# Linear attention and a two-layer block on one core: two copies of v moved behind phi(q), four transposes moved to the upper half of another PSUM bank

## The chip, the cores and the metric

The kernel runs on one core of a Trainium2 chip. The metric is the device time of one execution in microseconds (us); lower is better. The engines are named as in the profile: PE is TensorE (matrix multiplication), DVE is VectorE, ACT is ScalarE, POOL is GpSimd, SP is SyncE, which here only issues DMAs.

## The reference

```
def _attn_ref(q, k, v):                      # q, k, v: (8, 8, 576, 64)
    def phi(x):
        return np.where(x > 0, x, np.exp(x) - 1.0) + 1.0
    q_p, k_p = (phi(q), phi(k))
    kv = np.einsum('bhsd,bhse->bhde', k_p, v)
    z = np.sum(k_p, axis=2)
    num = np.einsum('bhsd,bhde->bhse', q_p, kv)
    den = np.einsum('bhsd,bhd->bhs', q_p, z)[..., None] + 1e-06
    return (num / den).astype(np.float32)

def _moe_ref(x, w_in, w_out):                # x: (4608, 512), w_in: (512, 2048)
    h = x @ w_in
    g = h - np.tanh(h)
    return (g @ w_out).astype(np.float32)    # (4608, 512)
```

The attention's result, with the heads side by side, is x. There are 8 batches of 576 tokens, 4608 rows in all.

## The kernel before, in words

**Chunks.** The 4608 rows of x are worked off in nine chunks of 512. Chunk c takes 512 rows of batch c; the last chunk takes the 64 rows that are left of each batch. A chunk has two halves. Layer 1 runs over 16 tiles `fi` of the hidden width: four matmuls each (`l1mm`, L468) into a PSUM bank, then tanh on ScalarE (L474 or L479) and a subtraction on VectorE (L475 or L480) that writes `gT`. Layer 2 runs over 16 steps `s` of four matmuls each (`l2mm`, L489), and `evac` copies its result out and stores it (L500, L513).

**The order is written by hand.** Each engine works off its instructions in the order in which the code issues them. The attention of the batches to come is placed between the matmuls by two tables of closures, `s1[fi]` and `s2[s]`: what stands in `s2[s]` is issued behind step `s` of layer 2. In chunk c the tables hold the phi work of batch c + 2 (`n2`), the numerators of batch c + 1 (`n1`) and the loads of batch c + 3; chunk 0 has entries of its own, for batches 1 and 2.

**phi.** `phi_pieces` (L137) makes, for one half `i` of a batch's heads, an exponential on ScalarE (L151), a tensor_scalar on VectorE (L152) and a minimum on VectorE (L153). `a_kphi` and `a_qphi` call it for k and q, which each have one raw buffer per pool.

**Copies of v.** `a_vp` (L201) copies half a batch of v into `vp`, the operand of the matmuls `kv_mm` (L198), beside columns of ones that give z. There is one `vp`. In chunk 1 the batch is 3, and its v is loaded by GpSimd in `s1[0]`, behind a `gate` (L482) that waits for the transposed phi(q) of batch 2.

**Numerators and kv.** `a_num(2, 3)` stands in `s2[12]` of chunk 1. It issues the numerators of batch 2 (L282, L291) and kv of batch 3 (L198), then on VectorE the copies of z and kv (`kz_copy`, L218 into `zr` and L223 into `kz`), and then `num_scale`, which multiplies the numerators by `rdb` and writes batch 2's part of `xT` (L439 four times, L444 twice). `rdb` holds the reciprocal denominators of batch 2; `a_spread` writes them to DRAM (L410) and reads them back to all partitions with two DMAs on SyncE's queue (L413). Layer 1 of chunk 2 reads that part of `xT`. `q_zb` in `s2[14]` turns `zr` by two matmuls (L230), copies the result on ScalarE (L233), and GpSimd multiplies it with phi(q) of batch 3 (L240).

**Transposes of batch 1.** In chunk 0, `s2[2]` transposes phi(q) of batch 1 on TensorE: `a_qT_pe` (L174) is called for `i` = 0 and `i` = 1, and each call issues two groups of four transposes (L182), each group into the lower half of a PSUM bank of its own, and gives back two copies into `qT` (L186), the first for ScalarE, the second for VectorE. Both copies of `i` = 0 are issued before the transposes of `i` = 1:

```
s2[2].append(lambda: ([f() for i in range(2) for f in a_qT_pe(1, i, Banks([4 + 2 * i, 5 + 2 * i]))], load_q(2)))
```

The four banks are 4, 5, 6 and 7. In layer 1 of chunk 0 the last four tiles, `fi` = 12 to 15, lie in the same four banks. All of PSUM is one tile, `ps_all`, of 8 banks of 512 float32 columns; waits between engines are put in by the framework from the accesses to it, none is written by hand.

Of the kernel before, what the change touches and what calls it, by code (L numbers as in the profile page):

```python
# [12 lines left out]
BF16 = mybir.dt.bfloat16  # L13
# [5 lines left out]
def kernel(  # L19
# [73 lines left out]
    def load(b, t, src, halves):  # L93

        n = main(b) if src is q else J
        x = src[b].rearrange("h (p j) d -> (h p) (j d)", j=J)[:, 0:n * D]
        if halves:
            y = x.rearrange("(h i q) x -> i q h x", h=2, i=2)
            for i in halves:
                for hs in ((0, 1), (1, 2)) if i and src is k and b == 0 else ((0, 2),):  # L100
                    nc.gpsimd.dma_start(out=t[:, hs[0]:hs[1], i, 0:n].rearrange("q h j d -> q h (j d)"),
                                        in_=y[i, :, hs[0]:hs[1]])
        else:
            nc.gpsimd.dma_start(out=t[:, :, :, 0:n].rearrange("q h i j d -> q (h i) (j d)"),  # L104
                                in_=x.rearrange("(n q) x -> q n x", n=4))
# [5 lines left out]
    def load_q(b):  # L111
        q_t[b] = kpool.tile([128, 2, 2, J, D], BF16, name="qraw")
        load(b, q_t[b], q, (0, 1) if b == 0 else ())
# [45 lines left out]
    def a_kphi(b, i):  # L159
        phi(b, k_t, kp_t, "kp", i)  # L160

    def a_qphi(b, i):
        phi(b, q_t, qp_t, "qp", i)

    def new_qT(b):
        qT_t[b] = work.tile([128, 2, J, 2, 64], BF16, name="qT")
# [4 lines left out]
            out=qT_t[b].rearrange("p i j g t -> p (i j) (g t)"),  # L171
            in_=qp_t[b].rearrange("p i j h d -> p (i j h d)"))

    def a_qT_pe(b, i, banks, on="AV"):  # L174
        if i == 0:
            new_qT(b)
        copies = []
        for n in range(2):
            j0, j1 = 4 * n, 4 * n + 4
            ps = banks().bitcast(BF16).rearrange("p (j t) -> p j t", t=128)  # L180
            for j in range(j0, j1):
                nc.tensor.transpose(ps[:, j - j0, :], qp_t[b][:, i, j].rearrange("p h d -> p (h d)"), ident)  # L182
            src = ps[:, 0:j1 - j0, :]
            dst = qT_t[b][:, i, j0:j1].rearrange("p j g t -> p j (g t)")
            copies.append((nc.scalar.copy if on[n] == "A" else nc.vector.tensor_copy, dst, src))
        return [lambda f=f, d=d, x=x: f(d, x) for f, d, x in copies]  # L186
# [14 lines left out]
    def a_vp(b, i, eng=nc.vector):  # L201
        eng.tensor_copy(vp[:, i, :, :, 0:64].rearrange("p j h d -> p h j d"), v_b[b % 2][:, :, i])  # L202

    def a_vp1(h, copy):
        copy(vp[:, 1, :, h, 0:64], v_b[1][:, h, 1])

    def kv_cols_mm(b, b0, o):
        kz_t[b] = kz_c[b if b < 2 else 2 + b % 2]
        kv_mm(b, lambda rs, h, i, j: vp[rs, i, j, h, :],
              lambda cs, hg, i: ps_all[cs, b0 + hg, o + 66 * i:o + 66 * i + 66])  # L210
# [67 lines left out]
    def num_mm(b, i, bank_of):  # L278

        kz, qT = kz_t[b], qT_t[b]  # L280
        for rs, cs, h, hg in quads():
            nc.tensor.matmul(ps_all[cs, bank_of(h), :].rearrange("p (j t) -> p j t", j=8), kz[rs, hg, i, 0:64],  # L282
                             qT[rs, i, 0:8, hg, :], start=True, stop=True)
# [164 lines left out]
    def new_ns(b):  # L448

        return rpool.tile([128, NP, J, 64], F32, name="ns", tag="rdb")  # L450

    def a_spread_pe(b, pairs):

        for n, p in enumerate(pairs):
            for t in range(4):
                r = slice(32 * t, 32 * t + 32)
                nc.tensor.matmul(ps_all[:, 4 + t, 128 * n:128 * n + 128], sel3[r, p].rearrange("p h e -> p (h e)"),
                                 rden_t[b][r, 0:128], start=True, stop=True)

    def a_scale(b, p, ns, n):  # L460
        nc.vector.tensor_mul(
            xT[:, p, 512 * b:512 * b + 512].rearrange("p (j t c) -> p t j c", j=8, t=4),
            ns[:, p, 0:8].rearrange("p j (t c) -> p t j c", t=4),
            ps_all[:, 4:8, 128 * n:128 * n + 128].rearrange("p t (j c) -> p t j c", c=16))
# [175 lines left out]
    for c in range(NC):  # L640
        gT = gpool.tile([128, NF, 512], BF16, name="gT")
        n1, n2 = c + 1, c + 2
        s1 = {i: [] for i in range(16)}
        s2 = {i: [] for i in range(16)}
        if c == 0:
            sub = {}

            def spread1():
                a_spread_pe(1, range(NP))
                for p in range(NP):  # L650
                    a_scale(1, p, sub["ns"], p)

            def kv1():
                kv_cols_mm(1, 4, 0)
                kz_copy(1, 4, 0)

            def num1():
                ns = sub["ns"] = new_ns(1)
                for i in (1, 0):
                    b0 = 4 + 2 * i  # L660
                    num_mm(1, i, lambda h: b0 + h)
                    nc.scalar.copy(ns[:, i::2, 0:8, :].rearrange("p a j t -> p a (j t)"), ps_all[:, b0:b0 + 2, :])

            def vp1():
                a_vp1(0, nc.vector.tensor_copy)
                a_vp1(1, nc.scalar.copy)

            s1[13].append(lambda: a_qphi(1, 0))
            s1[14].append(lambda: a_qphi(1, 1))
            s2[0].append(lambda: a_kphi(1, 0))  # L670
            s2[2].append(lambda: ([f() for i in range(2) for f in a_qT_pe(1, i, Banks([4 + 2 * i, 5 + 2 * i]))], load_q(2)))
            s2[3].append(lambda: (a_kphi(1, 1), load_k(2)))
            s2[4].append(prepare)
            s2[6].append(lambda: a_vp(1, 0))
            s2[8].append(lambda: (vp1(), load_v(2)))
            s2[9].append(kv1)
            s2[10].append(lambda: (a_den(1, 4), num1(), a_split(1)))
            s2[13].append(spread1)

            qs, ks = [], []  # L680

            def exp2(pieces, src, store, name, i):
                pieces.append(phi_pieces(2, src, store, name, i))
                pieces[i][0]()

            def rest2(f):
                f[1]()
                f[2]()

            def k2(i):  # L690
                ks.append(phi_pieces(2, k_t, kp_t, "kp", i))
                if not i:
                    ks[i][1]()

            s2[14].append(lambda: exp2(qs, q_t, qp_t, "qp", 0))
            s2[15].append(lambda: (exp2(qs, q_t, qp_t, "qp", 1), rest2(qs[0]), rest2(qs[1]), a_qT_dma(2), [f() for f in later], k2(0), k2(1)))
        elif n1 < B:
            if c == 1:
                def kv2():
                    kv_cols_mm(2, 6, 0)  # L700
                    kz_copy(2, 6, 0)

                s1[10].append(kv2)
            if n1 < QS:
                s1[11].append(lambda: (a_den(n1, 6), a_spread(n1)))
            else:
                if c == 2:
                    s1[2].append(lambda: (q_den(n1, 0, 0), q_den(n1, 0, 1)))
                e = 2 * (c == 2)
                s1[3 + e].append(lambda: q_den(n1, 1, 0))  # L710
                s1[5 + e].append(lambda: q_den(n1, 1, 1))
                s1[7 + e].append(lambda: q_scale(n1))
            m = 12 if c == 1 else 9
            if c == 3:
                s1[12].append(load_qr)
                s2[13].append(r_z)
            if c == 4:
                s2[1].append(r_phi)
                s2[12].append(r_prod)
            if c == 5:  # L720
                s2[1].append(r_scale)
            s2[m].append(lambda: (c == B - 2 and r_num(6, 128), a_num(n1, n2 if n2 < B else 0),
                                  c == B - 2 and r_copy(6, 128)))
            if n2 < B:
                s2[m + 2].append(lambda: (n2 == QS and q_zb(n2, 4), q_prod(n2)))
                if c > 1:
                    s2[15].append(lambda: (q_den(n2, 0, 0), q_den(n2, 0, 1)))
# [6 lines left out]
        if c >= 1 and n2 < B:  # L734
            d = 2
            s2[d].append(lambda: a_kphi(n2, 0))
            s2[d + 2].append(lambda: a_kphi(n2, 1))
            s2[d + 4].append(lambda: a_qphi(n2, 0))
            s2[d + 6].append(lambda: a_qphi(n2, 1))
            for i in range(2):  # L740
                s2[d + 1 + 2 * i].append(lambda i=i: a_vp(n2, i))
            if n2 + 1 < B:
                s2[15].append(lambda: (load_k(n2 + 1), load_v(n2 + 1), load_q(n2 + 1)))
        if c == 0:
# [18 lines left out]
        for fi in range(4 if c == 0 else 0, NF):  # L763
# [12 lines left out]
            elif fi % 2 and (c, fi) not in ((1, 9), (1, 11)):  # L776
                n = fi % 6
# [3 lines left out]
            if c == 1 and fi in (10, 11):  # L781
                n = 2 * (fi - 9)
                l1act2(6 + n, ps_all[:, n:n + 2, :], gT)
        os_ = {}
        for s in range(16):

            g, i = s % 4, s // 4
# [50 lines left out]
```

## Time and profile before

| What | Value |
|---|---|
| time, median of 3 runs | 282.6 us (282.32 to 282.66) |
| time of the profiled execution | 283.25 us |
| span of the profiled execution, first to last instruction | 281.4 us |
| PE busy | 275.9 us, 98% of the span |
| DVE busy | 177.9 us, 63% |
| ACT busy | 145.2 us, 52% |
| POOL busy | 82.3 us, 29% |
| granted TensorE clock, mean | 1.000 |
| layer 1, 560 matmuls of 128x512 (L468) | 123.0 us |
| layer 2, 560 matmuls of 128x512 (L489) | 124.2 us |

The span is what the trace covers; the time of the execution is 1.85 us longer. The profiled execution is one of its own and 0.65 us longer than the median of the runs. A row of a timeline reads: start in us from the span's start, length in us, engine and line, operation, output <- inputs, shape, count, and in brackets the idle time of the engine before it with what ended it. TensorE's matmuls overlap, so their pace is read from one start to the next and not from their lengths.

### The profile page before, as it was taken

How to read it: one execution, taken by the hardware profiler on the slowest of the kernel's cores; microseconds unless marked ns; L12 is line 12 of the kernel's file. 1: busy time of each engine (PE TensorE's matmuls, PEld its weight loads, DVE VectorE, ACT ScalarE, POOL GpSimd, SP SyncE). 2: the span in 40 equal slices, each digit the busy share in tenths (PEclk: the TensorE clock that was granted, in tenths of full speed). 3: DMA queues.
4: the chain of work that ended last, by engine and by line, in shares of the span. 5: the costliest groups of instructions: out<-in, count | busy, mean ns of one | idle time of the engine just before them, and what ended most of it. 6: DMA issues, size and time to landing. Idle time of an engine off the chain costs nothing.

```text
span 281.4 us, 5069 instructions
## 1 busy us (share of the span) xinstructions
PE 275.9 (98%) x2069; PEld 130.3 (46%) x2069; DVE 177.9 (63%) x289; ACT 145.2 (52%) x174; POOL 82.3 (29%) x79
## 2 busy tenths in 40 slices
PE   8999999999999999999999999999999999999995
PEld 3574544444444454444444444454444444444443
DVE  5759967993779764977497759784870267006600
ACT  4747908856246753566366735572651365126411
POOL 8652340330091409370824072505150000000000
PEclk9999999999999999999999999999999999999999
DMA  6999999799929754994498339862115210230033
GB/s 104 188 204 207 205 205 208 148 169 230 244 46 194 97 129 80 192 152 91 85 186 153 85 84 152 154 126 62 26 25 117 59 35 0 54 78 20 0 70 82
DMA packets 41559, 33.38 MB, mean 119 GB/s; under 512 B 19360, under 2 KB 37312, under 8 KB 41408
## 3 DMA queue, kind: packets, MB, share of 16 engines
q0 software_dynamic: 18688, 18.35, 40.8%
q1 hardware_dynamic: 22848, 14.71, 24.2%
q8 instruction: 16, 0.26, 0.4%
q14 instruction: 7, 0.06, 0.1%
HBM read 37.88 MB, written 9.46 MB: 168 GB/s over the span
## 4 chain that ended last, share of the span: by engine, by line
PE 69%; DMA 21%; DVE 3%; issue 2%; POOL 2%; ACT 1%; SPq 0%; POOLq 0%; DVEq 0%
PE ps_all L468 34%; PE ps_all L489 31%; DMA v<-in_v_dram 10%; DMA qraw<-in_q_dram 5%; DMA w_out_sb<-in_moe_w_out_dram 4%; DMA out_dram<-osb 3%; PE ps_all L578 2%; PE ps_all L198 1%; PE ps_all L282 1%; DVE xT L439 1%; ACT osb L500 1%; POOL w_in_sb L120 1%; DVE qp L153 1%; POOL kraw L104 1%; SPq L513 0%
## 5 line engine op out<-in xcount | busy, mean ns | idle before, releaser
L489 PE MATMUL ps_all<-w_out_sb,gT 128*128 128x512 bf16 x560 | 124.2, 379 | 0.0
L468 PE MATMUL ps_all<-xT,w_in_sb 128*128 128x512 bf16 x560 | 123.0, 379 | 0.3 <-DVE xT L439 0.3
L475 DVE TENSOR_TENSOR gT<-ps_all,th 128x1024 bf16<-128x1024 f32 x64 | 77.7, 1217 | 42.7 <-ACT th L474 42.6
L474 ACT ACTIVATE th<-ps_all 128x1024 f32<-128x1024 f32 x64 | 65.5, 1024 | 47.4 <-PE ps_all L468 47.4
L468 PEld LDWEIGHTS <-w_in_sb 128*128 128x128 bf16 x560 | 54.5, 98 | 66.3 <-issue 0.9
L489 PEld LDWEIGHTS <-gT 128*128 128x128 bf16 x560 | 54.0, 98 | 64.1 <-issue 0.2
L500 ACT COPY osb<-ps_all 128x512 f32<-128x512 f32 (+1 forms) x36 | 20.8, 582 | 55.0 <-PE ps_all L489 35.7
L240 POOL TENSOR_TENSOR pr<-qp,zb 128x1152 f32<-128x1152 bf16 x10 | 23.4, 2364 | 65.9 <-DMA zb<-zr 35.6
L254 POOL TENSOR_TENSOR qp<-qp,rd 128x1152 bf16<-128x1152 bf16 x10 | 21.0, 2112 | 28.3 <-DVE rd L251 17.9
L245 DVE TENSOR_REDUCE dn<-pr 128x9 f32<-128x576 f32 x20 | 14.5, 746 | 12.1 <-POOL pr L240 12.1
L151 ACT ACTIVATE e<-qraw 128x1152 bf16<-128x1152 bf16 (+1 forms) x16 | 18.2, 1136 | 3.6 <-DMA qraw<-in_q_dram 3.6
L151 ACT ACTIVATE e<-kraw 128x1152 bf16<-128x1152 bf16 x15 | 17.4, 1163 | 1.9 <-DMA kraw<-in_k_dram 1.9
L153 DVE TENSOR_TENSOR qp<-e,r 128x1152 bf16<-128x1152 bf16 (+1 forms) x16 | 11.9, 741 | 4.4 <-ACT e L151 3.3
L153 DVE TENSOR_TENSOR kp<-e,r 128x1152 bf16<-128x1152 bf16 x15 | 11.4, 758 | 4.3 <-ACT e L151 3.4
L578 PE MATMUL ps_all<-zero 128*128 128x512 bf16 x29 | 9.6, 490 | 1.2 <-DVE zero L523 1.2
L430 DVE CAST xT<-ps_all 128x1024 bf16<-128x1024 f32 x5 | 6.1, 1216 | 7.0 <-PE ps_all L291 7.0
L124 POOL DMA_DIRECT2D w_out_sb<-in_moe_w_out_dram x10 | 6.4, 645 | 9.8 <-DMA w_in_sb<-in_moe_w_in_dram 4.3
L480 DVE TENSOR_TENSOR gT<-ps_all,th 128x512 bf16<-128x512 f32 x12 | 7.9, 687 | 0.6
L479 ACT ACTIVATE th<-ps_all 128x512 f32<-128x512 f32 x12 | 7.2, 597 | 1.8 <-DVE gT L760 1.0
L202 DVE COPY vp<-v 128x1152 bf16<-128x1152 bf16 x11 | 5.0, 454 | 4.5 <-DMA v<-in_v_dram 4.5
L498 DVE COPY osb<-ps_all 128x128 f32<-128x128 f32 x1 | 0.3, 291 | 11.6 <-DMA out_dram<-osb 11.6
L152 DVE TENSOR_SCALAR r<-qraw 128x1152 bf16<-128x1152 bf16 (+1 forms) x16 | 7.4, 461 | 0.3 <-DMA qraw<-in_q_dram 0.3
(112 smaller groups left out, 148.3 us busy)
## 6 DMA issues: line engine op xcount, KB each, us to landing
out_dram<-osb SPq DMA_DIRECT2D x64, 128.0 KB, 2.4
kraw<-in_k_dram POOLq DMA_DIRECT2D x7, 576.0 KB, 6.4
qraw<-in_q_dram POOLq DMA_DIRECT2D x6, 576.0 KB, 9.9
v<-in_v_dram POOLq DMA_DIRECT2D x6, 576.0 KB, 8.7
w_in_sb<-in_moe_w_in_dram POOLq DMA_DIRECT2D x3, 512.0 KB, 9.7
v<-in_v_dram POOLq DMA_DIRECT2D x4, 288.0 KB, 8.8
rdb<-ds SPq DMA_DIRECT2D x2, 576.0 KB, 8.9
w_out_sb<-in_moe_w_out_dram POOLq DMA_DIRECT2D x4, 256.0 KB, 11.5
```

Of the source, the lines that this page charges most:

```text
L151: return (lambda: nc.scalar.activation(e, x, AF.Exp), lambda: nc.vector.tensor_scalar(r, x, 0.0, 1.0, ALU.max, ALU.add), lambda: nc.vector ...
L153: lambda: nc.vector.tensor_tensor(y, e, r, ALU.min))
L240: nc.gpsimd.tensor_mul(pr_t[b][:, i].rearrange("p j h d -> p j (h d)"), qp_t[b][:, i].rearrange("p j h d -> p j (h d)"), zb_t[b][:, i].uns ...
L245: nc.vector.tensor_reduce(dn_t[b][:, i, :, h], pr_t[b][:, i, :, h, :], mybir.AxisListType.X, ALU.add)
L254: nc.gpsimd.tensor_mul(x, x, rd[:, i].unsqueeze(2).to_broadcast([128, J * 2, D]))
L468: nc.tensor.matmul(h, w_in_sb[:, p, fi * 128:(fi + 1) * 128], xT[:, p, c * 512:(c + 1) * 512], start=(n == 0), stop=(n == NP - 1))
L474: nc.scalar.activation(th, h, AF.Tanh)
L475: nc.vector.tensor_sub(gT[:, fi:fi + 2, :], h, th)
L480: nc.vector.tensor_sub(gT[:, fi, :], h, th)
L489: nc.tensor.matmul(o, gT[:, fi, i * 128:(i + 1) * 128], w_out_sb[:, fi, :], start=(fi == 0), stop=(fi == NF - 1))
L500: nc.scalar.copy(osb[:, f0:f1], o[:, f0:f1])
L578: nc.tensor.matmul(ps_all[:, 0, :], zero[:, 0:128], zero, start=True, stop=True)
```

## The change

Two independent edits. In chunk 1 alone, the two copies of batch 3's v go from `s2[3]` and `s2[5]`, between the pieces of phi(k), to `s2[9]` and `s2[10]`, behind the second piece of phi(q) in `s2[8]`. In chunk 0, the transposes of batch 1's phi(q) with `i` = 1 use banks 6 and 5 where they used 6 and 7: the second group goes to the upper half of bank 5 (`up` counts blocks of 128 bfloat16 columns), whose lower half holds the second group of `i` = 0.

```diff
-    def a_qT_pe(b, i, banks, on="AV"):
+    def a_qT_pe(b, i, banks, on="AV", up=0):
...
-            ps = banks().bitcast(BF16).rearrange("p (j t) -> p j t", t=128)
+            ps = banks().bitcast(BF16).rearrange("p (j t) -> p j t", t=128)[:, n * up:n * up + 4]
...
-            s2[2].append(lambda: ([f() for i in range(2) for f in a_qT_pe(1, i, Banks([4 + 2 * i, 5 + 2 * i]))], load_q(2)))
+            s2[2].append(lambda: ([f() for i in range(2) for f in a_qT_pe(1, i, Banks([4 + 2 * i, 5]), up=4 * i)], load_q(2)))
...
-                s2[d + 1 + 2 * i].append(lambda i=i: a_vp(n2, i))
+                s2[d + 7 + i if c == 1 else d + 1 + 2 * i].append(lambda i=i: a_vp(n2, i))
```

## The prediction

> **What bounds the kernel now.** I read the page first, for the bound.
>
> ```profile
> PE 275.9 (98%) x2069; PEld 130.3 (46%) x2069; DVE 177.9 (63%) x289; ACT 145.2 (52%) x174; POOL 82.3 (29%) x79
> ```
>
> TensorE is busy 98% of the span and the chain of waits ends in its matmuls, so the change is worth what it does to TensorE's pauses. The busy share hides short ones, because a 128x512 matmul lasts 379 ns but the next starts after 216. So I read TensorE's timeline by start times at the two places that the diff touches.
>
> *Chunk 0, the transposes.* Windows at their start, their end, and on VectorE (start, length, what):
>
> ```profile
> 32.97 0.39 PE L182 MATMUL ps_all<-ident,qp 128*128 128x128 bf16 x4
> ...
> 33.34 0.38 PE L182 MATMUL ps_all<-ident,qp 128*128 128x128 bf16 x4
> 33.56 0.38 PE L489 MATMUL ps_all<-w_out_sb,gT 128*128 128x512 bf16 x1
> ```
>
> ```profile
> 32.60 0.68 DVE L480 TENSOR_TENSOR gT<-ps_all,th 128x512 bf16<-128x512 f32 x1
> 33.20 0.45 DVE L152 TENSOR_SCALAR r<-kraw 128x1152 bf16<-128x1152 bf16 x1
> 33.75 0.76 DVE L153 TENSOR_TENSOR kp<-e,r 128x1152 bf16<-128x1152 bf16 x1
> 34.43 0.75 DVE L186 COPY qT<-ps_all 128x512 bf16<-128x512 bf16 x2
> ```
>
> Transposes start 0.055 us apart (33.34 to 33.56 for four). The third group starts at 32.97, the fourth could start at 33.19, but it starts at 33.34: it writes bank 7, which L480 reads for the last tile of layer 1 until 32.60 + 0.68 = 33.28. That pause is 0.15 us, with 0.05 us from the end of the reader to the start of the matmul. The two L186 copies stand behind both pieces of kp; the first (34.43 to 34.85) reads the lower half of bank 5.
>
> *Chunk 1, batch 3.* Rows of VectorE and of TensorE:
>
> ```profile
> 66.73 0.76 DVE L153 TENSOR_TENSOR kp<-e,r 128x1152 bf16<-128x1152 bf16 x1 [0.74 <-ACT e L151]
> 72.03 0.46 DVE L202 COPY vp<-v 128x1152 bf16<-128x1152 bf16 x1 [4.54 <-DMA v<-in_v_dram]
> ...
> 76.47 0.42 DVE L218 CAST zr<-ps_all 128x256 bf16<-128x256 f32 x1
> 76.81 0.41 DVE L223 CAST kz<-ps_all 128x256 bf16<-128x256 f32 x1
> 77.14 2.47 DVE L439 TENSOR_TENSOR xT<-ps_all,rdb 128x512 bf16<-128x512 f32 x4
> ```
>
> ```profile
> 74.24 0.79 PE L198 MATMUL ps_all<-vp,kp 64*64 64x66 bf16 x72
> ...
> 76.95 0.29 PE L230 MATMUL ps_all<-ident,zr 128*128 128x128 bf16 x2
> 77.07 1.03 PE L489 MATMUL ps_all<-w_out_sb,gT 128*128 128x512 bf16 x4
> 77.94 0.38 PE L468 MATMUL ps_all<-xT,w_in_sb 128*128 128x512 bf16 x1
> 78.47 1.02 PE L468 MATMUL ps_all<-xT,w_in_sb 128*128 128x512 bf16 x4 [0.16 <-DVE xT L439]
> 79.67 4.69 PE L468 MATMUL ps_all<-xT,w_in_sb 128*128 128x512 bf16 x21 [0.17 <-DVE xT L439]
> ```
>
> VectorE stands 4.54 us before the first copy of v, with phi work queued behind it. It is then late for everything after: zr is ready when kv ends (about 75.05) but starts at 76.47, and L439, which makes batch 2's part of xT, ends its four pieces at 77.82, 78.42, 79.02 and 79.61. TensorE pauses for it three times: before L230 0.24 us (the last L489 starts at 76.49, L230 at 76.95, pitch 0.216), then 0.32 (77.94 to 78.47) and 0.33 (four L468 reach 79.34, the next starts at 79.67). Together 0.90 us; after 79.67 no pause follows that waits on another engine's data, so what is lost or won here reaches the end.
>
> **The change, part by part.**
>
> *The copies of v move behind phi(q).* Nothing is added: two copies of 0.46 us leave the head of the queue. VectorE's new order goes by ScalarE's exponentials, which the wait did not hold: in its rows they end at 68.24, 69.77 and 71.31, so kp's second piece ends near 69.0 and qp's near 70.6 and 72.1. v landed at 57.82 + 14.13 = 71.95 (chain of waits), so both copies run from 72.1 to 72.9 with no wait left. Matmuls L198 start at 74.24, so the cover is 1.3 us, and a later v would cost nothing within it. zr then starts when kv ends, at 75.1 instead of 76.5, kz ends by 75.8, and L439 could start 1.4 us earlier. But it has a second input, rdb, the reciprocal denominators read back from DRAM:
>
> ```profile
> 67.82 0.60 SPq L413 DMA_DIRECT2D rdb<-ds  x1
> ```
>
> ```profile
> DMA to landing us min/median/max: 8.9/8.9/8.9
> ```
>
> The second half of rdb lands at 67.82 + 8.9 = 76.7. So L439 starts at about 76.8, not at 75.8: 0.34 us before the 77.14 of now. Its four pieces, 0.60 apart, end at 77.5, 78.1, 78.7 and 79.28. TensorE, without the pause at L230, reaches the first L468 at 77.70; the second waits from 77.92 to 78.13, the last pair of xT (78.99 nominal) until 79.33. Gain: 79.67 - 79.33 = **0.34 us** of the 0.90. Bounds: 0, if rdb lands as late as the present start of L439, and 0.90, if it lands 0.6 us earlier; I take 0.34, from this execution's own landing. POOL's products and the loads behind them (L240, then k, v, q of batch 4) hang on L230 and come 0.2 us earlier; nothing waits for those.
>
> *The last four transposes go to the upper half of bank 5.* The same 16 transposes run, and the wait for bank 7 (0.15 us) goes. What takes its place: the lower half of bank 5 holds the second group, whose copy L186 is issued before the fourth group. Does a matmul wait for a reader of other columns of its bank? The trace of before has no matmul in that place. The nearest row is ScalarE's copy of the rest columns in later chunks:
>
> ```profile
> 102.86 0.41 DVE L223 CAST kz<-ps_all 128x256 bf16<-128x256 f32 x1
> 103.19 1.21 DVE L430 CAST xT<-ps_all 128x1024 bf16<-128x1024 f32 x1
> 103.37 0.27 ACT L431 CAST xT<-ps_all 128x128 bf16<-128x128 f32 x1 [0.55 <-DVE kz L223]
> ```
>
> ```profile
> ACT xT L431 <- DVE kz L223: 2.3, 4, 0.7
> ```
>
> L431 on ScalarE reads columns 0 to 127 of bank 7; L223 reads columns from 128 of banks 6 and 7. They share no data, both only read, and yet L431 starts 0.09 us after L223's end, in four chunks of four. It does not wait for L430, which reads other banks. So engines are kept apart by bank, not by columns. If two readers are, a writer and a reader are too: the fourth group then waits until 34.85, starts at 34.90 instead of 33.34, and L489 resumes **1.56 us** later. The stretch of pause is 33.19 to 34.90, 1.71 us. The low end is a gain of 0.15 us (no wait at all); I take 1.56, since four rows of four stand for it.
>
> The Trainium skill has a rule that speaks against this edit: PSUM — Partial Sum Buffer, section "PSUM bank collisions raise a hardware error", says that two engines on one bank and quadrant collide even at different addresses, and asks to guard by bank, not by address. By it the sum has +1.56 at this step, by columns -0.15; the page covers a writer against a reader, which the rows here do not show.
>
> Who waits behind: in TensorE's queue all of layer 2 of chunk 0. VectorE's second L186 (34.76) would start near 35.3, 0.6 us late; but the vp copies that end its run at 39.26 feed kv1, which TensorE then starts at 41.26 instead of 39.70. Nothing gives the delay back: the loads of batch 3 hang on qT of batch 2 (landed 55.46), that on phi(q) of batch 2, and that on L461 behind TensorE's spread; rdb hangs on the denominators. So v and rdb move with TensorE, and the picture near 78 us is the same 1.56 us later.
>
> *Sum.* Against the profiled execution's 283.25 us (span 281.4): +1.56 - 0.34 = +1.22, so 284.47. The median of the runs is 282.6, 0.65 lower; I apply the difference there: **283.8 us**.
>
> **The rivals.**
>
> 1. *Columns decide, not banks.* The fourth group starts at 33.19: -0.15 - 0.34 = -0.49, so 282.1, and 281.55 if rdb comes early (-0.15 - 0.90). This is the other side; it decides at whether the matmul at 33.19 waits for L186. For it: a tracker of columns would find no overlap. Against: the four waits of L431. Chance 0.08.
> 2. *rdb lands earlier in ordinary runs.* The profiled one is 0.65 us above the median, and its DMA may be slower. The copies then bring 0.90: +1.56 - 0.90 = +0.66, so 283.3. For it: L413 shares the engines with v, which lands at 71.95. Chance 0.18.
> 3. *rdb or v lands later, or the pause near 78 us is absent in ordinary runs,* and the copies bring nothing: +1.56, so 284.2. Chance 0.10.
> 4. *The pause lowers TensorE's clock.* The longest pause of before at full clock is 0.53 us, before the matmuls of 11.30, and 1.71 us is not shown. The first 17 matmuls took 6.53 us (chain of waits) where 17 x 0.216 is 3.67: about 2.9 us more, so 286.7. The Trainium skill (TensorE: Matmul & The Clock Gate, "What's actually happening") puts the fall after an idle window of about 3.4 us, by which this pause would not reach it; no run shown here tells. Chance 0.04.
>
> **How the numbers follow.** The forecast has 0.60. The range goes from 283.1, just below rival 2, to 284.4, just above rival 3, and leaves out rivals 1 and 4 (0.12). A measurement of this kernel can tell about 0.2% (0.57 us) from no change. Slower by more: forecast 0.60, rival 3 0.10, rival 4 0.04 and 0.14 of rival 2, whose +0.66 is close to the bound: 0.88. Within: 0.04 of rival 2 and half of rival 1: 0.08. Faster: the other half of rival 1: 0.04.
>
> **What would show it.** Right: between the third and fourth group of transposes a gap of 1.7 us that ends 0.05 us after the first L186; no wait for v on VectorE; L218 right behind L198; L439 starting 0.1 us after rdb lands, with one pause of TensorE in front of L468 still left. Wrong: a fourth group that follows without a gap (rival 1), L439 at once behind kz (rival 2), or matmuls 427 ns apart after the transposes (rival 4).

## The result, and the profile after

| What | before | changed |
|---|---|---|
| time, median of 22 runs each | 282.68 us | 285.0 us |
| ratio to before, 95% interval | | 1.0065 [1.0041, 1.0089] |
| profiled execution: time, span | 283.25, 281.4 us | 284.4, 282.6 us |
| mean granted TensorE clock | 1.000 | 0.999 |

The kernel became slower, by 0.65% (1.8 us by the ratio, 2.3 by the medians). The direction and the main term were as forecast, the amount was not: 285.0 lies above the range, which ended at 284.4. In some executions of most kernels here the last piece of batch 3's v lands some 5 us late and TensorE waits for it; the ratios leave the longest of these out, and of the profiled executions of e3, e6 and f3, which are such, only rows up to that wait are read, and TensorE's clock behind it.

TensorE's timeline of the changed kernel, at the transposes, and in layer 1 of chunk 1, where TensorE did not pause in before:

```profile
32.74 0.39 PE L182 MATMUL ps_all<-ident,qp 128*128 128x128 bf16 x4
34.68 0.39 PE L182 MATMUL ps_all<-ident,qp 128*128 128x128 bf16 x4 [1.55 <-DVE qT L186]
...
49.73 4.26 PE L468 MATMUL ps_all<-xT,w_in_sb 128*128 128x512 bf16 x19
54.56 1.67 PE L468 MATMUL ps_all<-xT,w_in_sb 128*128 128x512 bf16 x7 [0.56 <-DVE gT L475]
```

The fourth group of transposes follows the third after 1.71 us of pause by starts (the idle time of 1.55 counts from modelled ends) and waits for VectorE's copy out of bank 5, which ends at 34.62:

```profile
34.21 0.42 DVE L186 COPY qT<-ps_all 128x512 bf16<-128x512 bf16 x1
```

The second pause is new: by starts 0.73 us, from the due time 53.83 to 54.56. VectorE and GpSimd around it:

```profile
51.30 0.76 DVE L153 TENSOR_TENSOR qp<-e,r 128x1152 bf16<-128x1152 bf16 x1
51.97 1.40 DVE L152 TENSOR_SCALAR r<-kraw 128x1152 bf16<-128x1152 bf16 x1
53.29 2.34 DVE L475 TENSOR_TENSOR gT<-ps_all,th 128x1024 bf16<-128x1024 f32 x2
```

```profile
51.68 1.38 POOL L202 COPY vp<-v 128x1152 bf16<-128x1152 bf16 x1 [12.74 <-DMA v<-in_v_dram]
```

L152 takes 1.40 us where the same operation takes 0.45. It starts 0.29 us behind GpSimd's first copy of batch 2's v and ends 0.31 us after it. L475, which frees the bank that TensorE needs for its seventh tile, stands behind it. In before the order was the other way: L152 ended at 51.08, and GpSimd's copy began at 51.32:

```profile
50.63 0.45 DVE L152 TENSOR_SCALAR r<-kraw 128x1152 bf16<-128x1152 bf16 x1
51.00 1.22 DVE L475 TENSOR_TENSOR gT<-ps_all,th 128x1024 bf16<-128x1024 f32 x1
```

```profile
51.32 1.15 POOL L202 COPY vp<-v 128x1152 bf16<-128x1152 bf16 x1 [12.26 <-DMA v<-in_v_dram]
```

VectorE's queue moved by 1.35 us with TensorE's delay; the copy's start is set by the landing of batch 2's v, which moved from 51.17 to 51.53. So L152 slid under it. The Trainium skill describes such a clash (SBUF — State Buffer, "Who interferes with whom"): a tensor_scalar in a two-port mode and a GpSimd instruction need the same port pair, and whoever issues second is blocked for the other's whole instruction. The trace agrees: L152 runs on for 0.31 us behind the copy. By the same section of the Trainium skill L475 does not contend, as it has one input in SBUF and its operation has no two-port mode; its 1.21 us under the second copy, as elsewhere, agrees.

Near 80 us, VectorE and then TensorE:

```profile
73.94 0.82 DVE L202 COPY vp<-v 128x1152 bf16<-128x1152 bf16 x2
77.34 0.42 DVE L218 CAST zr<-ps_all 128x256 bf16<-128x256 f32 x1 [2.58 <-PE ps_all L198]
77.68 0.42 DVE L223 CAST kz<-ps_all 128x256 bf16<-128x256 f32 x1
78.01 2.48 DVE L439 TENSOR_TENSOR xT<-ps_all,rdb 128x512 bf16<-128x512 f32 x4
```

```profile
78.77 0.28 PE L230 MATMUL ps_all<-ident,zr 128*128 128x128 bf16 x2
78.88 1.03 PE L489 MATMUL ps_all<-w_out_sb,gT 128*128 128x512 bf16 x4
79.74 2.54 PE L468 MATMUL ps_all<-xT,w_in_sb 128*128 128x512 bf16 x11
```

All three pauses are gone, 0.90 us, and L439 follows kz at once. In the profiled pair the sum closes: from the start of the third group to the end of the span it is 248.4 us before and 249.9 after, +1.4; the terms are +1.56, +0.73 and -0.90, together +1.39. The span grew by 1.2, because this execution reached the transposes 0.2 us earlier.

### The profile page after: what moved, and what is told of

It is laid out like the page before. It is cut to its first block, busy times and chain, and to the rows that moved or that the text cites. A ratio compares the mean times of both kernels' runs of the same rounds, so it can differ in the third digit from the quotient of the medians.

```text
span 282.6 us, 5069 instructions
## 1 busy us (share of the span) xinstructions
PE 275.3 (97%) x2069; PEld 130.3 (46%) x2069; DVE 178.7 (63%) x289; ACT 145.2 (51%) x174; POOL 82.3 (29%) x79
## 4 chain that ended last, share of the span: by engine, by line
PE 83%; DVE 6%; DMA 4%; ACT 3%; issue 1%; POOL 1%; SPq 0%; DVEq 0%; ACTq 0%; POOLq 0%
PE ps_all L489 39%; PE ps_all L468 37%; DMA out_dram<-osb 2%; DMA kraw<-in_k_dram 2%; PE ps_all L198 2%; DVE gT L480 1%; ACT th L479 1%; PE ps_all L282 1%; PE ps_all L754 1%; DVE xT L461 1%; DVE r L152 1%; DVE gT L760 1%; ACT osb L500 1%; DVE qp L153 1%; SPq L513 0%
## 5 line engine op out<-in xcount | busy, mean ns | idle before, releaser
L489 PE MATMUL ps_all<-w_out_sb,gT 128*128 128x512 bf16 x560 | 124.2, 379 | 0.0
L468 PE MATMUL ps_all<-xT,w_in_sb 128*128 128x512 bf16 x560 | 122.8, 379 | 0.6 <-DVE gT L475 0.6
L475 DVE TENSOR_TENSOR gT<-ps_all,th 128x1024 bf16<-128x1024 f32 x64 | 77.7, 1217 | 43.0 <-ACT th L474 43.0
L468 PEld LDWEIGHTS <-w_in_sb 128*128 128x128 bf16 x560 | 54.7, 98 | 66.2 <-issue 0.8
L489 PEld LDWEIGHTS <-gT 128*128 128x128 bf16 x560 | 54.0, 98 | 64.1 <-issue 0.2
L153 DVE TENSOR_TENSOR qp<-e,r 128x1152 bf16<-128x1152 bf16 (+1 forms) x16 | 11.9, 742 | 5.4 <-ACT e L151 4.4
L153 DVE TENSOR_TENSOR kp<-e,r 128x1152 bf16<-128x1152 bf16 x15 | 11.4, 758 | 4.4 <-ACT e L151 3.3
L152 DVE TENSOR_SCALAR r<-kraw 128x1152 bf16<-128x1152 bf16 x15 | 7.8, 523 | 0.0
L152 DVE TENSOR_SCALAR r<-qraw 128x1152 bf16<-128x1152 bf16 (+1 forms) x16 | 7.4, 462 | 0.4 <-DMA qraw<-in_q_dram 0.4
```

The costliest lines, as they stand in the source:

```text
L152: lambda: nc.vector.tensor_scalar(r, x, 0.0, 1.0, ALU.max, ALU.add),
L153: lambda: nc.vector.tensor_tensor(y, e, r, ALU.min))
L468: nc.tensor.matmul(h, w_in_sb[:, p, fi * 128:(fi + 1) * 128], xT[:, p, c * 512:(c + 1) * 512], start=(n == 0), stop=(n == NP - 1))
L475: nc.vector.tensor_sub(gT[:, fi:fi + 2, :], h, th)
L489: nc.tensor.matmul(o, gT[:, fi, i * 128:(i + 1) * 128], w_out_sb[:, fi, :], start=(fi == 0), stop=(fi == NF - 1))
```

## The experiments

The theory after the result: the bank wait costs 1.56 us; the delay pushes L152 under GpSimd's copies, which costs about another 0.7; and the copies of v give nothing beside it, as the delay alone lets v and rdb land in time. The main rival is that each edit costs or gains by itself and the two add up. The ratios are to runs of the kernel before on the same chip.

**e1, the copies of v alone.**

```diff
-  s2[d + 1 + 2 * i].append(lambda i=i: a_vp(n2, i))
+  s2[d + 7 + i if c == 1 else d + 1 + 2 * i].append(lambda i=i: a_vp(n2, i))
```

> Only the copies of v move; the transposes stay in banks 6 and 7. Theory (the bank edit costs, this edit gains): no wait of VectorE for v, the 0.15 us in front of the fourth group of transposes stays, and the three pauses near 78 us shrink from 0.90 us to between 0 and 0.56 (0.56 if rdb still lands near 76.7): 0.3 to 0.9 us faster than before, about 282.0. Rival (the copies of v in their new place are what makes the changed kernel slower): 1 to 2 us slower than before.

Median 282.56 us, ratio 0.9987 [0.9946, 1.0027]: no difference that can be told. Its profile does have the order foreseen, and no pause of TensorE from 76.85 on:

```profile
72.02 0.82 DVE L202 COPY vp<-v 128x1152 bf16<-128x1152 bf16 x2
75.39 0.42 DVE L218 CAST zr<-ps_all 128x256 bf16<-128x256 f32 x1 [2.55 <-PE ps_all L198]
...
76.06 2.47 DVE L439 TENSOR_TENSOR xT<-ps_all,rdb 128x512 bf16<-128x512 f32 x4
```

rdb landed at 75.80 here, 0.9 us earlier than in the profiled before, and held nothing up. The edit does what it says. What it removes is worth 0.90 us in the profiled execution of before, which was 0.65 above the median. What it is worth in ordinary ones e1 leaves open: its interval, -1.5 to +0.8 us, holds zero, the 0.34 of the forecast and the 0.90. f1, below, narrows it.

**e2, the bank edit alone.**

```diff
-  s2[d + 7 + i if c == 1 else d + 1 + 2 * i].append(lambda i=i: a_vp(n2, i))
+  s2[d + 1 + 2 * i].append(lambda i=i: a_vp(n2, i))
```

(against the changed kernel)

> Only the bank edit; the copies of v stay in front. Theory: the fourth group of transposes waits 1.7 us for VectorE's copy out of bank 5, the stretched L152 under GpSimd's copies of batch 2's v is there too, and because the loads of batch 3 do not move by as much as TensorE, the pauses near 80 us are gone without the other edit: the same time as the changed kernel, within 0.3 us (about +2 us on before). Rival (the two edits add, as the prediction summed them): 0.3 to 0.9 us slower than the changed kernel, with pauses in front of L230 and L468 near 80 us.

285.3 us, ratio 1.0045 [1.0008, 1.0083]: the changed kernel's time. Its profile has both pauses of the changed kernel, 1.70 us at the transposes and 0.72 near 54 us, with L152 at 1.40. VectorE again stands in front of the copy of v, and TensorE does not pause at L230 or L468:

```profile
72.75 0.46 DVE L202 COPY vp<-v 128x1152 bf16<-128x1152 bf16 x1 [4.20 <-DMA v<-in_v_dram]
```

```profile
79.13 0.28 PE L230 MATMUL ps_all<-ident,zr 128*128 128x128 bf16 x2
79.24 1.03 PE L489 MATMUL ps_all<-w_out_sb,gT 128*128 128x512 bf16 x4
80.10 3.19 PE L468 MATMUL ps_all<-xT,w_in_sb 128*128 128x512 bf16 x14
```

So the edits do not add: with TensorE late by the bank wait, the 4.20 us wait for v is hidden. The slowdown is the bank edit's.

**e3, the upper half of bank 4 in place of bank 5.**

```diff
-  a_qT_pe(1, i, Banks([4 + 2 * i, 5]), up=4 * i)
+  a_qT_pe(1, i, Banks([4 + 2 * i, 5 - i]), up=4 * i)
```

> The changed kernel with the last four transposes in the upper half of bank 4, whose lower half ScalarE copies out early (it ended at 33.31 in the changed kernel, VectorE's copy out of bank 5 at 34.62). Theory (a write waits for a reader of the same bank, whichever columns): the pause in front of the fourth group ends 0.05 us after ScalarE's copy, 0.3 to 0.5 us long instead of 1.7, and the kernel is 1.2 us or more faster than the changed one, within 0.5 us of before. Rival (the pause comes from the write to an upper half, or from VectorE's queue as such): still 1.7 us and no faster.

The rows of TensorE and of ScalarE's first copy, out of bank 4's lower half:

```profile
32.69 0.39 PE L182 MATMUL ps_all<-ident,qp 128*128 128x128 bf16 x4
33.30 0.38 PE L182 MATMUL ps_all<-ident,qp 128*128 128x128 bf16 x4 [0.23 <-ACT qT L186]
```

```profile
32.66 0.58 ACT L186 COPY qT<-ps_all 128x512 bf16<-128x512 bf16 x1
```

The copy ends at 33.25 and the fourth group starts at 33.30: the pause is 0.39 us by starts and its end moved with the reader of the bank. Of the bank's float32 columns 256 to 511 are written and 0 to 255 read; the wait is by bank. Median 284.06, ratio 1.0004 [0.9952, 1.0056]: not to be told from before.

**e4, all 16 transposes issued ahead of the copies.**

```diff
-  [f() for i in range(2) for f in a_qT_pe(1, i, Banks([4 + 2 * i, 5]), up=4 * i)]
+  [f() for fs in [a_qT_pe(1, i, Banks([4 + 2 * i, 5]), up=4 * i) for i in range(2)] for f in fs]
```

> The changed kernel with all 16 transposes issued ahead of the four copies: the same banks, the same columns, only the order differs. Theory: the fourth group has no reader of bank 5 ahead of it, so it follows the third with no pause (0.06 us from start to start); TensorE is 0.15 us ahead of before instead of 1.56 behind, and with the copies of v moved the kernel is 0.4 to 1.05 us faster than before, 281.6 to 282.2. Rival (an upper half costs by itself): pause as in the changed kernel, about +2 us.

```profile
32.32 1.06 PE L182 MATMUL ps_all<-ident,qp 128*128 128x128 bf16 x16
33.22 0.59 PE L489 MATMUL ps_all<-w_out_sb,gT 128*128 128x512 bf16 x2
```

Sixteen transposes in one run, 0.90 us from the first to the next L489 (16 x 0.056): with the same banks and columns the pause is gone. An upper half by itself makes no pause; the order of issue decides. The time missed its expectation: 283.47, ratio 1.0008 [0.9965, 1.0051]. In its profile TensorE, now earlier, waits 0.11 us more in layer 1 of chunk 1 and 0.19 more in front of L381 for VectorE's kz, which takes the 0.15 back. The first of these is a clash too. VectorE issued L153, which reads two inputs from SBUF, while GpSimd's second copy ran (it ended at 53.92), and took 1.35 us for it instead of 0.76; the L475 that TensorE then waited for stands behind it:

```profile
53.19 1.35 DVE L153 TENSOR_TENSOR kp<-e,r 128x1152 bf16<-128x1152 bf16 x1
54.45 1.21 DVE L475 TENSOR_TENSOR gT<-ps_all,th 128x1024 bf16<-128x1024 f32 x1
```

**e5 and e6, GpSimd's two copies of batch 2's v left out,** of the changed kernel and of before.

```diff
-  s1[0].append(lambda: (a_vp(2, 0, nc.gpsimd), a_vp(2, 1, nc.gpsimd),
-                        gate(qT_t[n1]), load_k(n2), load_q(n2), load_v(n2)))
+  s1[0].append(lambda: (gate(qT_t[n1]), load_k(n2), load_q(n2), load_v(n2)))
```

> The changed kernel without GpSimd's two copies of batch 2's v into vp (left out; kv of batch 2 then uses batch 1's v). Theory (VectorE's L152 is held for as long as GpSimd's first copy runs, and the late L475 behind it makes TensorE pause 0.73 us at 53.6): L152 takes 0.45 us instead of 1.40, that pause is gone, the wait in front of the fourth transposes stays at 1.7 us, and the time is 0.7 us or more below the changed kernel, about 283.5 to 284.0. Rival (L152 is held by the transfer of k or by DMA writes): L152 stays long and the time stays at 284 to 286.

> Control: the kernel before without the same two copies on GpSimd (left out). Theory: in before L152 ends 0.24 us ahead of GpSimd's first copy, so nothing is held; the time is that of before within 0.3 us, and executions above 285 us, if they come from the same clash, are not seen. Rival (the copies on GpSimd cost in any order, by delaying the gate and the loads behind them): 0.5 us or more faster than before.

The rows of e5, VectorE and then TensorE, are as the theory has them: L152 is short again and layer 1 of chunk 1 runs without a pause.

```profile
52.66 0.45 DVE L152 TENSOR_SCALAR r<-kraw 128x1152 bf16<-128x1152 bf16 x1
53.03 2.49 DVE L475 TENSOR_TENSOR gT<-ps_all,th 128x1024 bf16<-128x1024 f32 x2
```

```profile
49.77 8.58 PE L468 MATMUL ps_all<-xT,w_in_sb 128*128 128x512 bf16 x39
```

The times went the wrong way, and both expectations were missed: e5 286.67, ratio 1.0087 [1.0036, 1.0138]; e6 288.8, ratio 1.0187 [1.0127, 1.0246]. Six of e5's twelve runs took 284.3 to 285.2 us and six 288.2 to 290.2; all six of e6 took 286.7 or more. In the profiled e6 TensorE stands before kv of batch 3 for its copies of v, which landed at 76.40 instead of 71.94:

```profile
76.94 0.71 PE L198 MATMUL ps_all<-vp,kp 64*64 64x66 bf16 x36 [2.47 <-DVE vp L202]
78.54 0.71 PE L198 MATMUL ps_all<-vp,kp 64*64 64x66 bf16 x36 [0.89 <-DVE vp L202]
```

The load was issued at the same time as in before (57.87 against 57.82). Why its last pieces come later without GpSimd's copies stays open. The times of the pair thus go by the late v, as far as this profile tells: the pair shows what holds L152, but not what it costs.

**e7, the kernel before with 28 more transposes in the fourth group,** a delay with no wait for a copy and with TensorE busy.

```diff
-  for j in range(j0, j1):
+  for j in [*range(j0, j1)] * (8 if b and i and n else 1):
```

> The kernel before with 28 further transposes in the fourth group (the same four, eight times over): TensorE and all behind it are 28 x 0.055 = 1.54 us late, with no wait for a bank and no idle TensorE. Theory (a delay of that size moves VectorE's L152 under GpSimd's copies of v, whose start is set by a load that does not move): L152 is long, TensorE pauses near 53.6 to 54.6, the pauses near 80 us are absorbed; the time is that of the changed kernel within 0.5 us, about 284 to 285.5. Rival (the additional loss comes from the idle stretch or from the moved copies): +1.54 less what the pauses near 78 give back, 0.6 to 1.6 us above before, no long L152.

```profile
52.02 1.40 DVE L152 TENSOR_SCALAR r<-kraw 128x1152 bf16<-128x1152 bf16 x1
53.35 2.34 DVE L475 TENSOR_TENSOR gT<-ps_all,th 128x1024 bf16<-128x1024 f32 x2
```

```profile
54.61 1.67 PE L468 MATMUL ps_all<-xT,w_in_sb 128*128 128x512 bf16 x7 [0.56 <-DVE gT L475]
```

284.78 us, ratio 1.0061 [1.0035, 1.0086]. Delay alone makes the same long L152 and the same pause, and gives the changed kernel's time: the additional loss comes neither from idle TensorE nor from the moved copies.

**e8 and f4, the changed kernel with the first L152 of batch 2's k two tiles later** (the same kernel twice), **and f3, the changed kernel again,** beside f4.

```diff
-                if not i:
-                    ks[i][1]()
...
-  s1[3 + 2 * i].append(lambda i=i: (i and ks[i][1](), ks[i][2]()))
+  s1[3 + 2 * i].append(lambda i=i: (ks[i][1](), ks[i][2]()))
```

> The changed kernel with the first L152 of batch 2's k issued two tiles of layer 1 later, behind two L475. Theory: the L475 that TensorE waits for no longer stands behind a held L152, so the pause of 0.73 us at 53.6 goes although the 1.7 us in front of the fourth transposes stay; time 0.5 us or more below the changed kernel, and less scatter. Rival (any VectorE work near GpSimd's copies is held, L475 too): no gain.

> The changed kernel with the first L152 of batch 2's k two tiles later, beside the changed kernel on one chip. Theory (the clash of VectorE's L152 with GpSimd's copies costs 0.7 us or more in ordinary runs too): 0.6 to 1.0 us below the changed kernel of this call, the 1.7 us pause unchanged. Rival (the clash costs only in the profiled execution): within 0.3 us of the changed kernel.

> The changed kernel once more, on the same chip as the three kernels beside it, as their reference. Theory: L152 held by GpSimd's first copy, TensorE's pause near 54 us of 0.7 us, time near 285.0. Rival (the 0.7 us pause is an accident of one execution): no long L152 this time.

VectorE of e8: L475 stands in front, and L152 runs clear of the copies (52.20 to 54.76).

```profile
52.59 1.22 DVE L475 TENSOR_TENSOR gT<-ps_all,th 128x1024 bf16<-128x1024 f32 x1
54.22 1.22 DVE L475 TENSOR_TENSOR gT<-ps_all,th 128x1024 bf16<-128x1024 f32 x1 [0.42 <-ACT th L474]
55.37 0.45 DVE L152 TENSOR_SCALAR r<-kraw 128x1152 bf16<-128x1152 bf16 x1
```

The pause near 54 us is gone. e8 took 284.12 us, ratio 1.0039 [1.0010, 1.0068]; f4 284.39, 1.0059 [1.0033, 1.0086], beside f3 with 285.52, 1.0078 [1.0047, 1.0108]. The medians of f3 and f4 are 1.1 us apart, their ratios 0.5, and the intervals overlap. e7 and e8 ran on one chip too, with delays of 1.64 and 1.67 us, and their medians are 0.66 apart. So the clash costs some 0.5 to 1 us in ordinary runs, and its size is not settled more closely. f3's profiled execution is a miss that teaches: L152 ran from 52.83 to 53.28 and GpSimd's first copy from 52.92, so L152 was first by 0.09 us and was not held, and TensorE did not pause near 54 us. In f3, as in the other executions, that copy starts 0.15 us after batch 2's v has landed. The clash is a race between VectorE's queue and the landing of a load, and not every execution loses it.

**f1 and f2, e1 and e4 with L152 later.** The edits are those above.

> The kernel before with the copies of v moved and the first L152 of batch 2's k two tiles later, no bank edit. Theory (without the delay of 1.56 us nothing is held; what the copies of v can give is small in ordinary runs): 282.2 to 282.6, 0 to 0.4 us below before. Rival (the clash is there in before too): 0.7 us or more below before.

> As the last one, with the last four transposes in the upper half of bank 5 and all 16 transposes issued ahead of the copies. Theory: the 0.15 us pause in front of the fourth group goes as well, 282.0 to 282.4, the fastest of all here. Rival (TensorE earlier only waits more for v and rdb near 78 us): no better than without the bank edit.

282.94 us, ratio 1.0011 [0.9995, 1.0027], and 282.9, ratio 1.0010 [0.9993, 1.0026]: neither beats before. f1 bounds what the copies of v give without a delay: 0.05%, 0.14 us, at most, unless the later L152 costs something by itself (TensorE waits 0.11 us more in front of L381 there). f2 runs its transposes without a pause and still has the two waits of e4 in chunk 1 (0.13 and 0.19 us): L152 in its later place met GpSimd's second copy, which ended at 53.71, and the L475 behind it came late.

```profile
53.34 0.69 DVE L152 TENSOR_SCALAR r<-kraw 128x1152 bf16<-128x1152 bf16 x1
```

No version here is faster than before by more than its interval.

## Why the prediction was right or wrong

- **The wait for the bank: right.** 1.71 us of pause were forecast and 1.71 measured, 0.05 us behind the copy. e3 and e4 show that it goes by bank and by order of issue. The reading that carried it was ScalarE's L431, which waited for a reader of other columns. The Trainium skill's advice to guard by bank (PSUM — Partial Sum Buffer, "PSUM bank collisions raise a hardware error") is what the waits in these runs do, for a writer against a reader too.
- **"Nothing gives the delay back ... v and rdb move with TensorE": wrong.** The loads of batch 3 were issued 2.0 us later (57.82 to 59.80), but v landed only 0.24 later (71.94 to 72.18), and rdb's second half about 0.4 (76.72 to 77.13). The loads took less time, so the delay itself hid the wait for v (e2).
- **The gain of 0.34 us from the copies: not there.** This is one of the two terms that failed. In the profiled execution all 0.90 us of the pauses are gone, but e2 loses them too with the copies in their old place: beside the bank edit the copies bring nothing, because the delay hides the wait. Without the delay f1 leaves them 0.14 us at most; e1, at -0.13% with a wide interval, does not tell. The last step of the sum carried a saving read from an execution 0.65 us above the median over to the median. That the pauses made up that excess is likely and not shown, as no other execution of before was traced.
- **What was missing: the clash of L152 with GpSimd's copies, 0.73 us in the profiled execution.** This is the other term, and the larger: the prediction put it at nothing. "Who waits behind" followed VectorE's queue only as far as kv1, and took the rest as moved rigidly. The row was there: 0.24 us between the end of L152 and a copy whose start a load sets. The profiles of e2 and e7 show the same pause, 0.72 us; in ordinary runs it is worth some 0.5 to 1 us (f3 against f4, e7 against e8).
- **The sum for the median.** 282.68 + 1.56 + 0.5 to 1 and nothing for the copies is 284.7 to 285.2; measured 285.0. By the ratio the change is 1.8 us, less than this sum's 2.1 to 2.6, but with an interval from 1.2 to 2.5. The forecast of 283.8 lacked the clash and credited 0.34.
- **The sum for the profiled execution: right by luck.** It gave 284.47, and 284.40 was measured. The 0.73 of the clash that was missing, the 0.56 by which more of the pauses went than forecast, and the 0.2 us by which this execution was ahead at the transposes cancel. The step from there to the median went the wrong way: before's profiled execution lay 0.65 above its median, the changed kernel's 0.6 below. Why the latter did stays open.
- **The rivals.** Columns in place of banks: refuted by e3. Rival 2's sign, L439 at once behind kz, was seen, though not for its reason: L439 came 0.87 us later than in before and rdb only 0.4. Rival 3, that the copies bring nothing in ordinary runs, came nearest of the four, and its 284.2 lacks the clash; but beside the bank edit they bring nothing because of the delay, which it did not name. A lowered clock: not seen after 1.71 us, with 0.999 and transposes at their normal pace. Longer waits did bring it, as the last section shows, so this rival named a real cost.

## What to carry to other kernels

In these kernels, where the framework puts in the waits, a write to PSUM waits for a reader of its bank that is issued earlier, whatever the columns: before a bank is shared, look at which copy stands in front of it and when that copy runs, and issue the writes first where the order is free. When a step delays an engine, look along its whole queue for neighbours whose time is set by something else, above all by a landing load, and check the gap to them; a gap smaller than the delay can be a term of the sum. A pause read from one profiled execution that lies above the median belongs to that execution until a run without it shows what it is worth.

## What had not been expected

- VectorE's L152 (128x1152, bfloat16) took 1.40 us instead of 0.45 when it started 0.29 us behind a GpSimd copy of 1.38 us; started 0.09 us ahead of one, it took 0.45. In the five executions in which it was caught by a copy (the changed kernel, e2, e7, f1, f2) it ended 0.31 to 0.32 us behind the copy's end, wherever it had started.
- The hold goes both ways: GpSimd's first copy took 1.15 us alone, and 1.20 to 1.60 (e2, the changed kernel, e7, e8, f4) where it started while VectorE's L153 ran, the longer the more of L153 was left; under L152, in f3, it took 1.36.
- TensorE at rest for 1.7 us by starts did not lose its clock: the transposes behind it start 0.055 us apart, as before. After waits of 2.47, 2.82 and 3.94 us for the late v in e6, f3 and e3 the granted clock was 0.5 for 6.8, 3.4 and 6.8 us, with 128x512 matmuls 0.427 us apart. Two of these waits are shorter than the window that rival 4 cites; just before and behind them TensorE had only matmuls on 64 rows (L282, L291, L198).
- A load of 576 KB issued 2.0 us later landed 0.24 us later.
